# Moving softmax sums, Wo and VectorE's MLP work to other slots of an attention schedule written out by hand

## The chip, the core and the metric

The kernel runs on one core of a Trainium2 chip. The metric is the device time of one execution in microseconds (us); lower is better. The engines that matter are TensorE (PE in the profile; PEld is its weight load), VectorE (DVE), ScalarE (ACT), GpSimd (POOL) and SyncE (SP). SP and POOL issue most of the DMA transfers. Each engine works through its own instructions in order; they meet at semaphores only.

## What is computed

With x of 2048 tokens by 512, 32 heads of 128, 2048 cached keys and values per head, and an MLP of inner width 1792:

```python
xn = layernorm(x)
# A: attention over a cache
q = (xn @ wq) in heads
p = softmax(q @ k_cache^T * 128 ** -0.5)
s = concat(p @ v_cache) @ wo
# B: mixer MLP
h = gelu(layernorm(xn) @ w1)
hs = (h, its four quarters shifted by +1, -1, +2, -2 tokens) @ w2
x1 = xn + hs
b = x1 + gelu(layernorm(x1) @ w3) @ w4
out = x + s * silu(b)
```

Everything in HBM is bf16; sums in PSUM are fp32; gelu is the tanh form.

## The kernel before

Attention is cut into 128 **units** of one head by 512 queries: eight groups of four heads, in each four blocks of queries, in each the four heads (`units`). A unit has eight **slots** (`SPU`). The main loop counts slots (n = 8u + p) and writes into each slot, by hand, what every engine gets; `pin` keeps that order on the engine, so the order of the program is the order of the work.

In slot p of unit u:

- `s_slot`: two score matmuls (tile ps_s, two buffers) for 256 keys, then one exp on ScalarE (L168) into half of a tile pT.
- `pv_slot`: two matmuls of probabilities by values (ps_o), five slots behind the scores (`LAG`).
- slots 0 and 1, `q_mm`: four matmuls of the next unit's queries (ps_q); slot 2, `q_copy`: VectorE takes them to SBUF (L155).
- VectorE adds up the exp tiles for the softmax sums: `add_first` in slot 4 (L174), `add_next` in slot 6 (L179), `add_last` in slot 0 of the next unit (L179, L184, L185).
- slot 3 of the next unit, `sums`: four matmuls with a column of ones (ps_sum), reciprocal on VectorE (L204), and a store of 2 KB to DRAM on SP's queue (dr, L206). Slot 4, `bcast`: SP reads it back spread over all partitions (rb, L210). Slot 2 of the unit after, `norm`: VectorE multiplies ps_o by rb into oT (L218).
- slots 4 and 5, `wo_mm`: two halves of one output projection (ps_wo, four matmuls in all) for a block whose four heads are normalized; slot 6, `wo_post`: VectorE adds it to s_acc (L244, L246), in the last head group also the final product and the store (L250, L252, L253).
- slots 2, 3 and 6, 7: one **chunk** of the MLP, two matmuls or more in each of the two slots (ps_m, one buffer). There are 136 chunks for 236 such windows, so most units have one: m1 (w1, with GELU), m2 (w2), m3 (w3, with GELU), m4 (w4). The chunk's later steps are put on a list for coming slots with `at(n, step)`, where n is the slot of the chunk's second half, 3 or 7 within a unit. They come at the end of their slot.

ps_q, ps_sum and ps_wo share one PSUM buffer (pool `psX`, tag `xa`): each waits until VectorE has read the one before.

The steps of two GELU chunks (`gelu_pair`) are: square on ScalarE at n+1 (L286), poly on VectorE at n+3 (L290), tanh on ScalarE at n+5 (L295), last on VectorE at n+7 (L298). m2 has x1 on VectorE at n+1 (L357) and statistics at n+2 (L363, L364); m4 has x2 on VectorE at n+1 (L451), tanh on ScalarE at n+3 (L455) and silu on VectorE at n+5 (L458). The second layernorm (`ln2`) is applied at n+8, 10, 12, 14 on VectorE (L393), each with a DMA transpose on SP (L396).

SP's queue also carries the transposing loads of K (`load_k`, L128): in the last four units of each head group but the last, two pieces in slot 5 and two in slot 7, at the top of the slot, ahead of what the slot has of attention. V, the weights and the stores between stages go through POOL's queue.

Of the kernel before, what the change touches and what calls it, by code (L numbers as in the profile page):

```python
# [17 lines left out]
def kernel(  # L18
# [35 lines left out]
    SPU = KC // 2  # L54
# [50 lines left out]
    def mm(out, lhsT, rhs, start, stop):  # L105
        pin(nc.tensor.matmul(out=out, lhsT=lhsT, rhs=rhs, start=start, stop=stop))  # L106
# [7 lines left out]
    NU = len(units)  # L114
# [4 lines left out]
    def at(n, fn):  # L119
        todo[n].append(fn)  # L120


    def load_k(h, pieces):
        w = Sk // KSPLIT
# [98 lines left out]
    def wo_mm(g, t, hhs):  # L223
        if hhs[0] == 0:
            wo_box[0] = psX.tile([P, D], FP32, tag="xa", name="ps_wo")
        oT = oTs[(g, t // 4)]
        ts = t % 4
        for hh in hhs:
            mm(wo_box[0][:], oT[:, hh, ts * P:(ts + 1) * P], wos[g * HG + hh][:], hh == 0, hh == HG - 1)
# [51 lines left out]
    def gelu_pair(pre, dest, n):  # L281
        sq = gtp.tile([P, 2, 512], BF16, name="sq")
        f2 = "p a f -> p (a f)"

        def square():
            pin(nc.scalar.activation(  # L286
                out=sq[:], in_=pre[:], func=ACT.Square, scale=GELU_A ** 0.5))

        def poly():
            pin(nc.vector.scalar_tensor_tensor(  # L290
                out=sq[:].rearrange(f2), in0=sq[:].rearrange(f2), scalar=1.0,
                in1=pre[:].rearrange(f2), op0=ALU.add, op1=ALU.mult))

        def tanh():
            pin(nc.scalar.activation(out=sq[:], in_=sq[:], func=ACT.Tanh, scale=GELU_C))  # L295

        def last():
            pin(nc.vector.scalar_tensor_tensor(  # L298
                out=dest, in0=sq[:], scalar=1.0, in1=pre[:], op0=ALU.add, op1=ALU.mult))

        at(n + 1, square)
        at(n + 3, poly)
        at(n + 5, tanh)
        at(n + 7, last)

    def gelu_chunk(lhs, rhs, j, key, dest):
        def run(i, n):
# [36 lines left out]
    def m2_chunk(t):  # L344
        def run(i, n):
            if i == 0:
                mlp["ps"] = psX.tile([P, 512], FP32, tag="xm", name="ps_m")
                mlp["xr"] = tokp.tile([P, D], BF16, tag="tb", name="xr")
                nc.gpsimd.dma_start(out=mlp["xr"][:], in_=xn_d[t][:])
            for jc in (2 * i, 2 * i + 1):  # L350
                c0 = BASE_J[jc] + t * P - SHIFT[jc]
                mm(mlp["ps"][:], hT[:, jc, c0:c0 + P], w2_sb[:, jc, :], jc == 0, jc == DC - 1)
            if i == 1:
                ps, xr = mlp["ps"], mlp["xr"]

                def x1():
                    pin(nc.vector.scalar_tensor_tensor(  # L357
                        out=xr[:], in0=ps[:], scalar=0.5, in1=xr[:], op0=ALU.mult, op1=ALU.add))
                    nc.gpsimd.dma_start(out=x1_d[t][:], in_=xr[:])

                def stats():
                    bn = smp.tile([P, nc.vector.BN_STATS_DIM], FP32, name="bn")
                    pin(nc.vector.bn_stats(out=bn[:], in_=xr[:]))  # L363
                    pin(nc.vector.bn_aggr(out=mv2[:, t, :], in_=bn[:]))  # L364
                    rsqrt(rstd2[:, t:t + 1], mv2[:, t, 1:2])

                at(n + 1, x1)
                at(n + 2, stats)
        return run

    def ph2_open():
# [8 lines left out]
    def ln2(c, n):  # L380
        def start():
            mlp["xn2T"] = mp.tile([P, DC, 512], BF16, name="xn2T")
            xs = []
            for ts in range(4):
                xr = tokp.tile([P, D], BF16, tag="ta", name="x1r")
                nc.gpsimd.dma_start(out=xr[:], in_=x1_d[c * 4 + ts][:])
                xs.append(xr)
            mlp["xs"] = xs

        def apply(ts):  # L390
            t = c * 4 + ts
            xr = mlp["xs"][ts]
            pin(nc.vector.tensor_scalar(  # L393
                out=xr[:], in0=xr[:], scalar1=mv2[:, t, 0:1], scalar2=rstd2[:, t:t + 1],
                op0=ALU.subtract, op1=ALU.mult))
            pin(nc.sync.dma_start_transpose(  # L396
                out=mlp["xn2T"][:, :, ts * P:(ts + 1) * P], in_=xr[:]))

        at(n, start)
        for ts in range(4):  # L400
            at(n + 8 + 2 * ts, lambda ts=ts: apply(ts))

    def m3_chunk(c, fc):
        def dest():
# [28 lines left out]
    def m4_chunk(t, part):  # L433
        fcs = list(M4[part])
        ts = t % 4

        def run(i, n):
            if part == 0 and i == 0:
                mlp["ps"] = psX.tile([P, 512], FP32, tag="xm", name="ps_m")
                mlp["xr"] = tokp.tile([P, D], BF16, tag="tb", name="xr")  # L440
                nc.gpsimd.dma_start(out=mlp["xr"][:], in_=x1_d[t][:])
            h = (len(fcs) + 1) // 2
            for fc in (fcs[:h], fcs[h:])[i]:
                mm(mlp["ps"][:], mlp["h2"][fc // 2][:, fc % 2, ts * P:(ts + 1) * P],
                   mlp["w4"][fc][:], fc == 0, fc == FC - 1)
            if part == 2 and i == 1:
                ps, xr = mlp["ps"], mlp["xr"]
                th = tokp.tile([P, D], BF16, tag="th", bufs=1, name="th")

                def x2():  # L450
                    pin(nc.vector.scalar_tensor_tensor(  # L451
                        out=xr[:], in0=ps[:], scalar=0.5, in1=xr[:], op0=ALU.mult, op1=ALU.add))

                def tanh():
                    pin(nc.scalar.activation(out=th[:], in_=xr[:], func=ACT.Tanh, scale=0.5))  # L455

                def silu():
                    pin(nc.vector.scalar_tensor_tensor(  # L458
                        out=xr[:], in0=th[:], scalar=1.0, in1=xr[:], op0=ALU.add, op1=ALU.mult))
                    nc.gpsimd.dma_start(out=g_d[t][:], in_=xr[:])  # L460

                at(n + 1, x2)
                at(n + 3, tanh)
                at(n + 5, silu)
        return run

    chunks = deque()
# [47 lines left out]
    wo_todo = deque()  # L515
    for n in range(NS + 3 * SPU):
        u, p = divmod(n, SPU)
        if u < NU:
            g, qt, hh = units[u]
            if g + 1 < NG and qt == QT - 1:  # L520
                h = (g + 1) * HG + hh
                if p == 5:
                    load_k(h, (0, 1))
                elif p == 6:
                    load_v(h)
                    load_w(h)
                elif p == 7:
                    load_k(h, (2, 3))
                    load_wo(h)
            s_slot(u, p)  # L530
        m = n - LAG
        if 0 <= m < NS:
            pv_slot(*divmod(m, SPU))
        if p in (0, 1) and u + 1 < NU:
            q_mm(u + 1, (2 * p, 2 * p + 1))
        if p == 0 and 1 <= u <= NU:
            add_last(u - 1)
        if p == 2 and u + 1 < NU:
            q_copy(u + 1)
        if p == 2 and 2 <= u <= NU + 1:  # L540
            norm(u - 2)
            if units[u - 2][2] == HG - 1:
                gg, qq = units[u - 2][:2]
                wo_todo.extend((gg, 4 * qq + ts) for ts in range(4))
                if gg == NG - 1:
                    fin_load(4 * qq)
        if p == 3 and 1 <= u <= NU:
            sums(u - 1)
        if p == 4 and 1 <= u <= NU:
            bcast(u - 1)  # L550
        if p in (4, 5) and wo_todo:
            wo_mm(*wo_todo[0], (0, 1) if p == 4 else (2, 3))
        if p == 6 and wo_todo:
            gg, t = wo_todo.popleft()
            wo_post(gg, t)
            if gg == NG - 1 and t % 4 < 3:
                fin_load(t + 1)
        if p == 4 and u < NU:
            add_first(u)
        if p == 6 and u < NU:  # L560
            add_next(u, 2)
        if p in (2, 3, 6, 7):
            w = 2 * u + (p >= 4)
            i = p % 2
            if i == 0:
                want = -(-(w + 1 - W0) * NCH // (W1 - W0)) if w >= W0 else 0
                window.pop("run", None)
                if done < min(want, NCH):
                    if done in hooks:
                        hooks.pop(done)(n)  # L570
                    window["run"] = chunks.popleft()
                    done += 1
            if "run" in window:
                window["run"](i, n)
        for fn in todo.pop(n, ()):
            fn()
# [37 lines left out]
```

## Time and profile before

| | us |
|---|---|
| three timed runs | 1322.03, 1326.29, 1327.14 |
| their median | 1326.29 |
| the profiled execution | 1323.47 |
| its span, first to last instruction | 1321.7 |
| busy in it: PE, ACT, DVE | 1270.7, 1112.5, 1024.5 |
| mean granted TensorE clock | 0.991 |

The page counts an engine's busy time as a union of its instructions. Matmuls are pipelined: one of 128x512 shows some 380 ns, but the next starts 0.216 us after it. So a delay of TensorE is read from starts, not from gaps. In the list of waits a row says who waited, for whom, how long in all, how often and the longest.

### The profile page before, as it was taken

How to read it: one execution, taken by the hardware profiler on the slowest of the kernel's cores; microseconds unless marked ns; L12 is line 12 of the kernel's file. 1: busy time of each engine (PE TensorE's matmuls, PEld its weight loads, DVE VectorE, ACT ScalarE, POOL GpSimd, SP SyncE). 2: the span in 40 equal slices, each digit the busy share in tenths (PEclk: the TensorE clock that was granted, in tenths of full speed). 3: DMA queues.
4: the chain of work that ended last, by engine and by line, in shares of the span. 5: the costliest groups of instructions: out<-in, count | busy, mean ns of one | idle time of the engine just before them, and what ended most of it. 6: DMA issues, size and time to landing. Idle time of an engine off the chain costs nothing.

```text
span 1321.7 us, 17163 instructions
## 1 busy us (share of the span) xinstructions
PE 1270.7 (96%) x6208; PEld 575.4 (44%) x6208; DVE 1024.5 (78%) x1402; ACT 1112.5 (84%) x1185; POOL 220.2 (17%) x356
## 2 busy tenths in 40 slices
PE   3899999999999999999999999999999999999995
PEld 1344444444444444444444444444444444444442
DVE  1898788888787877788877777888777888777886
ACT  2799988778999988899988889998888999888882
POOL 6630122333211021100111011001010100000101
PEclk9899999999999999999999999999999999999997
DMA  9741373234823267222652127423292312712223
GB/s 217 189 102 27 53 140 84 72 85 112 151 57 70 55 116 124 61 41 44 127 114 60 48 49 121 96 56 65 62 146 57 64 33 48 132 29 52 81 67 88
DMA packets 144468, 112.29 MB, mean 85 GB/s; under 512 B 112320, under 2 KB 114880, under 8 KB 144384
## 3 DMA queue, kind: packets, MB, share of 16 engines
q1 hardware_dynamic: 126496, 57.19, 25.0%
q0 software_dynamic: 17600, 53.76, 15.8%
q8 instruction: 48, 0.79, 0.3%
q14 instruction: 36, 0.29, 0.1%
q10 hardware_dynamic: 288, 0.26, 0.1%
HBM read 81.53 MB, written 8.65 MB: 68 GB/s over the span
## 4 chain that ended last, share of the span: by engine, by line
PE 79%; DVE 9%; ACT 6%; DMA 3%; issue 2%; POOL 1%; DVEq 0%; POOLq 0%; SPq 0%
PE ps_s L106 29%; PE ps_o L106 27%; PE ps_m L106 8%; PE ps_wo L106 8%; PE ps_q L106 6%; ACT pT L168 4%; DVE acc L179 3%; PE ps_sum L106 1%; DVE acc L184 1%; DVE qT L155 1%; ACT sq L286 1%; DMA rb<-dr 1%; DMA xin<-in_A_x_dram 1%; ACT pre L316 1%; DVE gl L250 1%
## 5 line engine op out<-in xcount | busy, mean ns | idle before, releaser
L168 ACT ACTIVATE pT<-ps_s 128x1024 bf16<-128x1024 f32 x1024 | 1015.8, 1029 | 183.0 <-PE ps_s L106 179.0
L106 PE MATMUL ps_s<-qT,kT 128*128 128x512 bf16 x2048 | 611.2, 380 | 5.0 <-DVE qT L155 2.7
L106 PE MATMUL ps_o<-pT,vb 128*128 128x512 bf16 x2048 | 610.0, 380 | 0.0
L179 DVE TENSOR_TENSOR acc<-acc,pT 128x2048 bf16<-128x2048 bf16 x256 | 312.5, 1221 | 75.2 <-ACT pT L168 70.0
L106 PEld LDWEIGHTS <-vb 128*128 128x128 bf16 x2048 | 200.0, 98 | 243.0 <-issue 1.9
L106 PEld LDWEIGHTS <-kT 128*128 128x128 bf16 x2048 | 196.4, 98 | 244.2 <-issue 26.8
L174 DVE TENSOR_TENSOR acc<-pT 128x2048 bf16<-128x2048 bf16 x128 | 156.0, 1219 | 30.9 <-ACT pT L168 30.8
L106 PE MATMUL ps_q<-xnT,wq_h 128*128 128x512 bf16 x512 | 153.9, 383 | 20.7 <-DMA xnT<-xn 20.7
L106 PE MATMUL ps_wo<-wo_h,oT 128*128 128x512 bf16 x512 | 155.2, 387 | 7.4 <-DVE s_acc L246 3.1
L246 DVE TENSOR_TENSOR s_acc<-ps_wo,s_acc 128x512 f32<-128x512 f32 x112 | 77.3, 690 | 97.9 <-PE ps_wo L106 97.9
L155 DVE CAST qT<-ps_q 128x512 bf16<-128x512 f32 x128 | 87.3, 682 | 12.3 <-PE ps_q L106 12.3
L184 DVE TENSOR_TENSOR acc<-acc 128x1024 bf16<-128x1024 bf16 x128 | 88.6, 692 | 4.4
L218 DVE TENSOR_TENSOR oT<-ps_o,rb 128x512 bf16<-128x512 f32 x128 | 87.2, 681 | 4.6 <-DMA rb<-dr 4.5
L106 PEld LDWEIGHTS <-wq_h 128*128 128x128 bf16 x512 | 50.3, 98 | 81.9 <-DMA wq_h<-in_A_wq_dram 20.7
L106 PEld LDWEIGHTS <-oT 128*128 128x128 bf16 x512 | 50.6, 99 | 73.4 <-issue 14.5
L106 PE MATMUL ps_m<-xn2T,w_sb 128*128 128x512 bf16 x224 | 66.5, 378 | 0.0
L428 POOL DMA_DIRECT2D w_sb<-in_B_w_dram x28 | 21.2, 757 | 264.0 <-PE ps_m L106 235.1
L106 PE MATMUL ps_m<-w_sb,h2T 128*128 128x512 bf16 x224 | 63.9, 379 | 0.0
L139 POOL DMA_DIRECT2D wq_h<-in_A_wq_dram x32 | 24.5, 767 | 219.7 <-PE ps_q L106 217.1
L185 DVE TENSOR_TENSOR acc<-acc 128x512 bf16<-128x512 bf16 x128 | 54.4, 425 | 4.4
L106 PEld LDWEIGHTS <-acc 128*128 128x128 bf16 x512 | 37.2, 116 | 45.7 <-issue 14.7
L134 POOL DMA_DIRECT2D vb<-in_A_v_cache_dram x32 | 37.4, 1167 | 114.9 <-PE ps_o L106 104.6
(51 smaller groups left out, 607.1 us busy)
## 6 DMA issues: line engine op xcount, KB each, us to landing
rb<-dr SPq DMA_DIRECT2D x128, 256.0 KB, 4.1
vb<-in_A_v_cache_dram POOLq DMA_DIRECT2D x32, 512.0 KB, 7.1
w_sb<-in_B_w_dram POOLq DMA_DIRECT2D x28, 256.0 KB, 4.4
wq_h<-in_A_wq_dram POOLq DMA_DIRECT2D x32, 128.0 KB, 3.1
wo_h<-in_A_wo_dram POOLq DMA_DIRECT2D x32, 128.0 KB, 4.3
kT<-in_A_k_cache_dram SPq DMA_TRANSPOSE x128, 4.8
xn_d<-xn POOLq DMA_DIRECT2D x16, 128.0 KB, 3.9
dr<-rc SPq DMA_DIRECT2D x128, 2.0 KB, 1.5
```

What stands on the lines that cost most here:

```text
L106: pin(nc.tensor.matmul(out=out, lhsT=lhsT, rhs=rhs, start=start, stop=stop))
L134: nc.gpsimd.dma_start(out=vBs[h][:], in_=A_v_cache[0, h].rearrange("(kc p) d -> p kc d", p=P))
L139: nc.gpsimd.dma_start(out=wqs[h][:], in_=wq_v[:, :, h * Dh:(h + 1) * Dh])
L155: pin(nc.vector.tensor_copy(out=qT[:], in_=st[u].pop("psq")[:]))
L168: pin(nc.scalar.activation(out=s["pT"][-1][:, jj:jj + 2, :], in_=sps[:], func=ACT.Exp, scale=SCALE))
L174: pin(nc.vector.tensor_tensor(out=s["acc"][:], in0=s["pT"][0][:], in1=s["pT"][1][:], op=ALU.add))
L179: pin(nc.vector.tensor_tensor(out=a[:], in0=a[:], in1=st[u]["pT"][i][:], op=ALU.add))
L184: pin(nc.vector.tensor_tensor(out=a[:, 0:2, :], in0=a[:, 0:2, :], in1=a[:, 2:4, :], op=ALU.add))
L185: pin(nc.vector.tensor_tensor(out=a[:, 0, :], in0=a[:, 0, :], in1=a[:, 1, :], op=ALU.add))
L218: pin(nc.vector.tensor_tensor(out=oTs[(g, qt)][:, hh, :], in0=s["o"][:], in1=s["rb"][:], op=ALU.mult))
L246: pin(nc.vector.tensor_tensor(out=sa, in0=ps[:], in1=sa, op=ALU.add))
L428: nc.gpsimd.dma_start(out=w[:], in_=w3_v[:, :, fc * P:(fc + 2) * P])
```

## The change

The sums move from slot 3 to 4, their broadcast from slot 4 to 5, the two halves of Wo from slots 4 and 5 to 5 and 6; `wo_post` stays in slot 6, after the second half. VectorE's statistics, layernorm applies and silu are rounded up to the next slot 3, 5 or 7 (`soft`); x1 and x2 come in the chunk's own slot if that is slot 7, else one slot later as before (`evict`); GELU's poly, tanh and last come at n+4, n+6, n+8.

```diff
+    def soft(n):
+        while n % SPU not in (3, 5, 7):
+            n += 1
+        return n
+
+    def evict(n):
+        return n if n % SPU == SPU - 1 else n + 1
...
         at(n + 1, square)
-        at(n + 3, poly)
-        at(n + 5, tanh)
-        at(n + 7, last)
+        at(n + 4, poly)
+        at(n + 6, tanh)
+        at(n + 8, last)
...
-                at(n + 1, x1)
-                at(n + 2, stats)
+                at(evict(n), x1)
+                at(soft(n + 2), stats)
...
         for ts in range(4):
-            at(n + 8 + 2 * ts, lambda ts=ts: apply(ts))
+            at(soft(n + 8 + 2 * ts), lambda ts=ts: apply(ts))
...
-                at(n + 1, x2)
+                at(evict(n), x2)
                 at(n + 3, tanh)
-                at(n + 5, silu)
+                at(soft(n + 5), silu)
...
-        if p == 3 and 1 <= u <= NU:
+        if p == 4 and 1 <= u <= NU:
             sums(u - 1)
-        if p == 4 and 1 <= u <= NU:
+        if p == 5 and 1 <= u <= NU:
             bcast(u - 1)
-        if p in (4, 5) and wo_todo:
-            wo_mm(*wo_todo[0], (0, 1) if p == 4 else (2, 3))
+        if p in (5, 6) and wo_todo:
+            wo_mm(*wo_todo[0], (0, 1) if p == 5 else (2, 3))
         if p == 6 and wo_todo:
             gg, t = wo_todo.popleft()
             wo_post(gg, t)
```

## The prediction

> **What bounds the kernel.** I read the busy shares first, then PE's waits, then the timeline of single units. A unit (one head, 512 queries) has eight slots; numbers below are slot numbers, U is the start of a unit's first score matmul.
>
> The page's first part and clock row:
>
> ```profile
> PE 1270.7 (96%) x6208; PEld 575.4 (44%) x6208; DVE 1024.5 (78%) x1402; ACT 1112.5 (84%) x1185; POOL 220.2 (17%) x356
> ...
> PE   3899999999999999999999999999999999999995
> ...
> PEclk9899999999999999999999999999999999999997
> ```
>
> TensorE is the bound: 5696 matmuls of 128x512 that start 0.216 us apart when nothing holds them take 1230 us alone. So only PE's waits can be won, and only new ones lost. PE's waits over the whole span:
>
> ```profile
> PE ps_q L106 <- DMA xnT<-xn: 20.7, 1, 20.7
> PE ps_sum L106 <- DVE qT L155: 9.7, 15, 3.6
> PE ps_wo L106 <- DVE s_acc L246: 3.1, 4, 0.8
> PE ps_s L106 <- DVE qT L155: 2.7, 2, 1.9
> PE ps_wo L106 <- DVE oT L218: 2.5, 1, 2.5
> PE ps_sum L106 <- DVE acc L185: 2.5, 2, 2.2
> ```
>
> The first is the start. The second is what the change aims at: the sums in slot 3 need the one `xa` PSUM buffer, which q_copy frees in slot 2. A modelled matmul hides the first 0.16 us of a wait, so I counted delays from start to start in the timeline: up to the tail the sums lose 14.7 us (unit 1 alone 3.76), Wo in slot 4 3.4 us, and scores that wait for an exp some 11 us, mostly in pieces of 0.1 to 0.2. One such wait, DVE and PE at the end of slot 3 of unit 22:
>
> ```profile
> 251.32 0.68 DVE L357 SCALAR_TENSOR_TENSOR xr<-ps_m,xr 128x512 bf16<-128x512 f32 x1
> 252.04 0.69 DVE L363 BATCH_NORM_STATS2 bn<-xr 128x6 f32<-128x512 bf16 x1
> 252.77 0.18 DVE L364 BATCH_NORM_AGGREGATE mv<-bn 128x2 f32<-128x6 f32 x1
> 252.87 0.66 DVE L155 CAST qT<-ps_q 128x512 bf16<-128x512 f32 x1
> ```
>
> ```profile
> 252.49 0.59 PE L106 MATMUL ps_o<-pT,vb 128*128 128x512 bf16 x2
> 253.58 0.27 PE L106 MATMUL ps_sum<-ones_t,acc 128*128 128x1 bf16 x4 [0.50 <-DVE qT L155]
> ```
>
> The columns are start, duration, engine, line. After two ps_o the sums could start at 252.49 + 0.43 = 252.92; they start at 253.58, when the copy's 252.87 + 0.66 is over: 0.66 lost. x1 and the statistics (1.55 us by starts) stand ahead of the copy.
>
> **Part by part.** No arithmetic is added or removed; instructions move.
>
> *Slot lengths.* Scores and PV take 0.863 us, each pair of other matmuls 0.43, the sums 0.125. Before, slots 4 and 5 carry Wo; now 5 and 6. Wo's second half stands in slot 6 ahead of the MLP pair. So from the end of Wo to the next sums PE does the same work as before: six slots of scores and PV, two q pairs, the MLP pairs (old slots 6 to 3, new 6 to 4). **Where VectorE is gated by Wo's result (s_acc, L246), the shift alone wins nothing**: everything moves by one slot. It wins where VectorE is gated by an exp, or by what the second edit takes off the road.
>
> *MLP stage 2 (160 to 330 us).* Trace it through a unit with MLP in slots 6, 7 (unit 23). New Wo's second half starts at U+7.46; s_acc started 0.63 us after it before (255.87, 256.50), so U+8.09. By steps between starts: s_acc 0.61, add 1.14 gives x1 at 9.84; its matmul is out at 9.81, so the new wait in slot 7 is nothing. Queued behind x1 is the add of the last exp tile, ready at 10.03; it starts at 10.56. Then 1.26 + 0.72 + 0.34 gives q_copy at 12.88, done at 13.54. The sums come at U+9.62+5.18 = 14.80: 1.2 us to spare. Behind the copy come norm 0.60 and stats 0.82; the reciprocal could run at 14.87 and waits for the sums until 15.1; Wo starts at 15.79. The waits of units 17, 18, 22, 23, 24, 25, 29 go: 0.66+0.23+0.66+0.66+0.98+0.23+0.66 = **4.1 us**. Unit 16's (0.85 + 0.83) I keep: there the last GELU step and the statistics both stand before its reciprocal, so Wo waits. Wo of unit 30 (1.24, a late rb) I count at **0.9**; ends 0 and 1.24.
>
> *Six units (47, 52, 67, 72, 92, 112)* lose 0.20 at the sums (silu, 0.68, ahead of the copy) and 0.12 in slot 1 (tanh after short slots 6 and 7). Silu goes to slot 3 or 5, slot 6 gets longer: **1.9 us**.
>
> *Last units.* Unit 120's 0.83 falls to the 0.34 of its successors (silu again): **0.5**. The 0.34 of units 121 to 126 is the s_acc loop and stays.
>
> *Start.* Unit 1's sums wait 3.76 us because VectorE stands behind a load (DMA xin, 9.6 us). One slot later the wait is 2.9. After it PE runs at half speed (starts 0.427 apart) up to 48.2; the windows view gives a clock of 1.00 in 30 to 40 us and 0.66 in 40 to 50. A 2.0 us wait ending at 34.5 left full speed, the 3.76 us one did not; 2.9 lies midway. I take full speed, at little better than even odds. That is worth 2.7 to PE (13 matmuls, 0.21 late each), but only the 1.8 for which VectorE waited for the exp before 49.66. Units 2 and 4 lose 0.26 and 1.02; VectorE is nearly full there (9.9 of 10 us in 60 to 70), so 0.7 of it. Together **2.5**, ends 0.7 and 4. The 0.86 of lead is given back at the end, where s_acc of unit 127 comes 0.86 later and the last adds follow it.
>
> The Trainium skill, "TensorE: Matmul & The Clock Gate", The HAM clock gate, says that the clock halves after one idle window of about 3.4 us. The row with 3.76 us agrees, the tail's half speed after a 2.3 us wait does not; by the rule 2.9 us would keep the clock and the sum stays; by the tail's row the sum below is 1.8 less.
>
> *ScalarE.* A score matmul waits for the exp two slots back. From its start to the exp's end is 1.75 us by the rows (0.69 to the exp's start, 1.02, 0.04), exps follow each other at 0.905, a GELU tanh adds 0.95. Unit 9 shows the squeeze with the tanh in slot 0:
>
> ```profile
> 119.77 1.07 ACT L295 ACTIVATE sq<-sq 128x1024 bf16<-128x1024 bf16 x1
> ...
> 120.72 3.79 ACT L168 ACTIVATE pT<-ps_s 128x1024 bf16<-128x1024 f32 x4
> ...
> 121.80 0.59 PE L106 MATMUL ps_s<-qT,kT 128*128 128x512 bf16 x2
> 121.81 0.10 PEld L106 LDWEIGHTS <-kT 128*128 128x128 bf16 x1 [0.33 <-issue]
> ```
>
> Loss 0.22. With the tanh in slot 1 and slots 2, 3 bare (no sums in 3), the slack before slot 3 is 1.295+0.863-1.75 = 0.41, then 0.41+0.863-1.855 = -0.58. By the chunk schedule five pairs end in slot 3 with that pattern after them (units 8, 15, 34, 41, 100); unit 16 hides its own. They lost 0.1 to 0.2 before, so 0.38 more, four times: 1.5. Thirteen pairs that end in slot 7 with bare slots 2, 3 after them lose 0.05 each in slot 4 (0.905 against 0.863): 0.7. **Cost 2.2**, ends 0 and 4.
>
> *SyncE and DMA.* In the built program's order the broadcast rb passes behind two K transposes in 28 units (four per head group but the last), which it preceded before; the reciprocal's store dr stays ahead. Before:
>
> ```profile
> 173.37 0.32 SPq L206 DMA_DIRECT2D dr<-rc  x1
> 174.78 0.32 SPq L210 DMA_DIRECT2D rb<-dr  x1
> 175.15 6.12 SPq L128 DMA_TRANSPOSE kT<-in_A_k_cache_dram  x4
> ```
>
> Two transposes hold SP until dr+2.75 (1.1 and 1.3 us); rb went at dr+1.4 to 3.5 in these units before, so it is 0 to 1.3 us later, but with two transposes behind it in place of four. It took 3.9 to 7.7 there, mostly 5 to 6, and 4.1 in the median of all. So rb lands at dr+6.9 to 9.5, likely 7.3. Norm needs it at 13.45 against dr at 5.7, or 7.8 later, and 0.75 us more is covered, by VectorE's wait for the sums (15.1 - 14.87) and Wo's spare 0.5. Price nothing in most units; I take **0.7**, ends 0 and 27 (28 times 0.95). The V load from POOL's queue runs beside it as before.
>
> The Trainium skill speaks against this edit: "DMA: Bandwidth & Descriptors", Queues, rings and completion order, says a ring's descriptors are consumed in order, so rb could not overtake the transposes. Before, no rb stands behind a transpose issued just ahead of it, so the trace is silent. By the rule rb waits for the second transpose, issued at dr+1.5 and landed 4.8 later by the median, and the sum stays; with the slowest landing of these units (6.7) all 28 would be late and the sum about zero.
>
> *Sum*: 4.1+0.9+1.9+0.5+2.5 = 9.9 won, 2.2+0.7 lost: **7.0 us**. The profiled execution took 1323.47 (span 1321.7, 1.8 around it), so 1316.5 for its like; the median of the three runs shown, 1326.29, lies 2.8 higher, and from it 1319.3. That is the forecast.
>
> *At nothing*: GELU's poly, tanh and last step one slot later (the first reader of the result is at least one chunk, four slots, on; without it one slot, 1.3 us, per pair), and layernorm 2's applies with their four transposes on SP one to three slots later (eight stage-2 or twelve stage-4 chunks hide them; without these up to 3.9 us, four times). x1 and x2 in slot 7 free the MLP's PSUM buffer earlier, which no matmul waited for.
>
> **Rivals.**
> 1. *The wait only changes its name.* The closed loop through s_acc, reciprocal and Wo is the real limit, Wo waits where the sums did, and the start stays at half speed. For: VectorE waits 97.9 us for Wo before L246, and that loop is as long as before. Against: it waits 70.0 us for exps before L179, in stage 2 above all (0.96 ahead of the add at 259.28). Won 4.1/2 + 1.9 + 0.7 = 4.7, lost 2.2 + 0.7: gain 1.8, 1324.5.
> 2. *More is won.* Stage 2 in full (7.0 with units 16 and 30), start 4, rest 2.4, ScalarE free: gain 13, 1313.
> 3. *Slower: rb behind the transposes.* If it lands more than 8.55 us after dr, norm is late, the reciprocal behind it on VectorE too, and Wo waits. At the worst bound, dr+9.5, each of 28 units loses 0.95, 27 us; less the 7.7 won otherwise, 1345; with half the units, 1332. For: rb took up to 7.7 once and Wo then waited 1.24. Against: norm had over 1 us to spare in most units.
>
> **Numbers.** Forecast case (gain 4.5 to 10) 0.50; rival 1 0.28; rival 2 0.12; rival 3 0.10. The range 1311 to 1327 leaves out rival 3 and the rim of rival 2. A measurement tells 0.5%, 6.6 us: 1319.7. Of the forecast case 0.36 lies beyond it, with rival 2 faster 0.48; same 0.14+0.28 = 0.42; slower 0.10.
>
> **What will show it.** In the waits, ps_sum on qT falls from 9.7 to under 5 us, with none in stage 2; clock near 1.00 in 40 to 50 us; ps_s waits of some 0.5 us in slot 4 of units 9, 35, 42, 101; ps_sum waits of 0.34 (0.2 in the view) from unit 121 on. Wrong if ps_wo on rc or oT on rb grow to several us, or the sums' wait stays.

## The result and the profile after

The changed kernel takes **1330.48 us** (median of 7 runs, 1328.08 to 1333.55); the kernel before, beside it, 1322.03 (7 runs, 1321.20 to 1327.14). The ratio is 1.0055, 95% interval 1.0040 to 1.0069: slower by some 7 to 8 us, where 7.0 faster was forecast. The profiled execution took 1333.55 (span 1331.4), the longest of the seven.

The page's busy line and the two rows of slices, in the order shown of before:

```profile
PE 1265.0 (95%) x6085; PEld 576.1 (43%) x6208; DVE 1013.6 (76%) x1402; ACT 1108.3 (83%) x1185; POOL 223.8 (17%) x356
...
PE   3899999999999999999999999999999999999995
...
PEclk9999999999999999999999999999999999999996
```

TensorE is still the bound and its work is the same. (This trace lacks 123 of the 6208 matmul records; where one is missing, the next seems 0.216 us late, with nothing that released it.) VectorE is busy 76% instead of 78% of a longer span. The waits of PE over the whole span tell more:

```profile
PE ps_o L106 <- DVE oT L225: 7.8, 8, 1.8
PE ps_s L106 <- ACT pT L175: 5.1, 15, 0.7
PE ps_wo L106 <- DVE rc L211: 4.4, 9, 0.8
PE ps_sum L106 <- DVE qT L162: 3.6, 3, 2.7
```

Line numbers are seven higher than before. The sums' wait for the query copy fell from 9.7 us in 15 places to 3.6 in 3, all three in the first 80 us: from there on the wait that the change aims at is gone. In its place stands a row that the kernel before does not have, PV (ps_o) waiting for norm (oT) 7.8 us. Wo's wait for the reciprocal rose to 4.4 us; before, it was

```profile
PE ps_wo L106 <- DVE rc L204: 1.7, 2, 1.1
```

Both hang on VectorE, whose own waits say why:

```profile
DVE rc L211 <- PE ps_sum L106: 88.4, 82, 2.5
DVE oT L225 <- DMA rb<-dr: 36.7, 24, 2.7
```

Before, these two were

```profile
DVE rc L204 <- PE ps_sum L106: 30.7, 51, 1.2
DVE oT L218 <- DMA rb<-dr: 4.5, 3, 2.2
```

The first row says that VectorE now comes to the reciprocal before the sums are there. The second is the one that costs: norm waits for rb. The prediction had named this row as a sign that it is wrong.

**Unit 22**, whose 0.66 us the prediction showed, in the changed kernel: VectorE's copy and statistics, and PE's sums.

```profile
251.02 0.68 DVE L162 CAST qT<-ps_q 128x512 bf16<-128x512 f32 x1
...
252.22 0.68 DVE L370 BATCH_NORM_STATS2 bn<-xr 128x6 f32<-128x512 bf16 x1
```

```profile
253.00 0.26 PE L106 MATMUL ps_sum<-ones_t,acc 128*128 128x1 bf16 x4
```

The statistics now stand behind the copy, the copy ends at 251.70, and the sums start 1.3 us after it without a wait (1.2 was predicted for unit 23, where it is 1.4).

**Where the time comes from.** I laid the start of each unit's first exp beside that of before. By unit 28 the changed kernel is 3.2 us ahead. Then it falls back in steps: it is level at units 48 to 60, 3.7 behind at 80, 7.8 at 84, 8.4 at 96, and 8.8 at the end. Nearly every step lies where the next head group's K is loaded (units 28 to 31, 44 to 47, 60 to 63, 76 to 79, 92 to 95), or in the few units behind it, where the norms of these units stand. Such a place is unit 78, whose dr and rb go in unit 79 and whose norm stands in unit 80. First SP's queue, then VectorE, then PE, last the windows view (its column behind the engines is the granted clock):

```profile
827.46 0.32 SPq L213 DMA_DIRECT2D dr<-rc  x1
827.87 3.34 SPq L135 DMA_TRANSPOSE kT<-in_A_k_cache_dram  x2
833.15 0.32 SPq L217 DMA_DIRECT2D rb<-dr  x1
```

```profile
838.30 0.69 DVE L225 TENSOR_TENSOR oT<-ps_o,rb 128x512 bf16<-128x512 f32 x1 [2.56 <-DMA rb<-dr]
...
840.04 0.18 DVE L211 RECIPROCAL rc<-ps_sum 128x4 f32<-128x4 f32 x1
```

```profile
839.04 0.59 PE L106 MATMUL ps_o<-pT,vb 128*128 128x512 bf16 x2 [1.62 <-DVE oT L225]
840.27 1.01 PE L106 MATMUL ps_wo<-wo_h,oT 128*128 128x512 bf16 x2 [0.63 <-DVE rc L211]
```

```profile
841.00:844.00 3.00, 3.00 (x10) 1.15 (x9) 0.63 (x2) 1.02 (x1) 0.00 (x0) 0.61 0.23 44
```

Read downwards: dr is issued, two transposes at once behind it; SP is free of them at 831.2, but dr lands only at 833.13, 5.7 us after its issue, and rb, which reads what dr wrote, goes at 833.15 and lands at 838.27. Norm stood ready since 835.74. PV of unit 80 needs the PSUM buffer that norm reads, and waits; the reciprocal stands behind norm on VectorE, so Wo waits; and the clock is 0.61 in the mean of the 3 us behind these gaps: the trace's clock record has half speed from 839.93, within the second gap, to 843.34. In the changed kernel rb lands 10.8 us after dr's issue. In the kernel before it landed 7.4 us after it, with dr down in 1.6:

```profile
822.73 0.52 SPq L206 DMA_DIRECT2D dr<-rc  x1
824.34 0.32 SPq L210 DMA_DIRECT2D rb<-dr  x1
```

### The profile page after: what moved, and what is told of

It is laid out like the page before. It is cut to its first block, busy times and chain, and to the rows that moved or that the text cites. A ratio compares the mean times of both kernels' runs of the same rounds, so it can differ in the third digit from the quotient of the medians.

```text
span 1331.4 us, 17063 instructions
## 1 busy us (share of the span) xinstructions
PE 1265.0 (95%) x6085; PEld 576.1 (43%) x6208; DVE 1013.6 (76%) x1402; ACT 1108.3 (83%) x1185; POOL 223.8 (17%) x356
## 4 chain that ended last, share of the span: by engine, by line
PE 73%; DMA 9%; DVE 8%; ACT 7%; issue 2%; SPq 1%; POOL 1%; DVEq 0%; ACTq 0%; POOLq 0%
PE ps_s L106 26%; PE ps_o L106 25%; PE ps_m L106 8%; PE ps_wo L106 8%; PE ps_q L106 6%; ACT pT L175 5%; DMA rb<-dr 4%; DMA dr<-rc 3%; DVE acc L186 2%; PE ps_sum L106 1%; ACT sq L293 1%; SPq L135 1%; DMA xin<-in_A_x_dram 1%; DVE acc L191 1%; ACT pre L323 1%
## 5 line engine op out<-in xcount | busy, mean ns | idle before, releaser
L106 PE MATMUL ps_s<-qT,kT 128*128 128x512 bf16 x2002 | 600.9, 380 | 10.1 <-ACT pT L175 5.1
L106 PE MATMUL ps_o<-pT,vb 128*128 128x512 bf16 x1999 | 598.4, 379 | 10.8 <-DVE oT L225 7.8
L106 PEld LDWEIGHTS <-kT 128*128 128x128 bf16 x2048 | 192.4, 98 | 231.2 <-issue 33.9
L181 DVE TENSOR_TENSOR acc<-pT 128x2048 bf16<-128x2048 bf16 x128 | 153.0, 1195 | 0.3
L211 DVE RECIPROCAL rc<-ps_sum 128x4 f32<-128x4 f32 x128 | 22.9, 179 | 88.5 <-PE ps_sum L106 88.4
L192 DVE TENSOR_TENSOR acc<-acc 128x512 bf16<-128x512 bf16 x128 | 54.4, 425 | 4.4
```

The source lines that it names most:

```text
L181: pin(nc.vector.tensor_tensor(out=s["acc"][:], in0=s["pT"][0][:], in1=s["pT"][1][:], op=ALU.add))
L192: pin(nc.vector.tensor_tensor(out=a[:, 0, :], in0=a[:, 0, :], in1=a[:, 1, :], op=ALU.add))
L211: pin(nc.vector.reciprocal(out=rc[:], in_=ps[:]))
```

## The experiments

The theory after this reading: **the two K transposes between dr and rb in 28 units cost what was lost and more; the rest of the change is a gain.** Rivals: the slots of the sums and Wo cost by themselves, or ScalarE's later tanh does. Each kernel was timed beside the kernel before in five rounds; ratios are to that, with 95% intervals.

### rb ahead of the transposes (e1)

```diff
-                if p == 5:
-                    load_k(h, (0, 1))
...
         if p == 5 and 1 <= u <= NU:
             bcast(u - 1)
+        if p == 5 and u < NU and g + 1 < NG and qt == QT - 1:
+            load_k((g + 1) * HG + hh, (0, 1))
```

> The changed kernel with one thing undone: in slot 5 the two K transposes are issued behind the broadcast rb, so that SP's order is dr, rb, four transposes as before the change. Theory (rb late behind the transposes): the waits of norm on rb fall from 36.7 us in 24 places to under 8 us, the waits of ps_o on norm go except at the start, and the time falls from 1330 by 10 to 15 us, to 2 to 8 us below the kernel before. Rival (the moved sums and Wo, or the shorter slots 3 and 4, cost the time by themselves): it stays within 3 us of the changed kernel, 5 to 9 us above the kernel before.

Measured: 1321.94 us (1319.33 to 1324.54, 12 runs), ratio 0.9986 [0.9973, 0.9998]. That is 8.5 us less than the changed kernel's median, or 0.69% by the two ratios, 9.1 us, where I expected 10 to 15. Norm still waits 14.6 us for rb, in 17 places; I expected under 8. SP in the same unit:

```profile
818.43 0.52 SPq L213 DMA_DIRECT2D dr<-rc  x1
821.75 0.32 SPq L217 DMA_DIRECT2D rb<-dr  x1
822.12 5.03 SPq L135 DMA_TRANSPOSE kT<-in_A_k_cache_dram  x4
```

PE's waits from 60 to 1230 us, past the start and ahead of the tail, for e1:

```profile
PE ps_s L106 <- ACT pT L175: 3.7, 11, 0.4
PE ps_wo L106 <- DVE rc L211: 1.2, 2, 0.8
PE ps_sum L106 <- DVE qT L162: 0.5, 1, 0.5
```

In that view the changed kernel has

```profile
PE ps_o L106 <- DVE oT L225: 6.0, 7, 1.6
PE ps_wo L106 <- DVE rc L211: 4.0, 8, 0.8
```

with ps_s at 4.1 and ps_sum at 0.4. PV's wait is gone, Wo's mostly. So this order is the cause of the loss. But the kernel is only 1.8 us faster than before, at the low end of the 2 to 8 that I expected.

### Each part alone (e2, e3, e4)

e2 is the kernel before with the broadcast alone in slot 5, behind the transposes; e3 has the first edit alone, e4 the second alone (`soft`, `evict`, GELU one slot later).

```diff
-        if p == 4 and 1 <= u <= NU:
+        if p == 5 and 1 <= u <= NU:
             bcast(u - 1)
```

> The kernel before with one thing changed: the broadcast rb is issued in slot 5, behind the two K transposes, and sums and Wo stay in slots 3 to 5. Theory: rb lands 1 to 3 us later in 28 units; norm has 0 to 2 us more room than in the changed kernel, so the price is smaller than there but clear: 4 to 12 us above the kernel before. Rival: the place of rb in SP's queue is hidden, within 2 us of the kernel before.

Measured: 1329.11 us, ratio 1.0043 [1.0028, 1.0058]. Norm waits 20.0 us for rb (before 4.5), Wo 5.4 for the reciprocal (1.7). The order in SP's queue alone costs 5.4 us, with the sums still in slot 3.

> The first edit alone: sums, broadcast and Wo one slot later, VectorE's MLP work as before. Theory: the price of rb is in it, the win in MLP stage 2 mostly is not: as slow as the changed kernel or up to 5 us slower, 7 to 14 us above the kernel before. Rival (the second edit is what costs): within 3 us of the kernel before.

Measured: 1331.65 us, ratio 1.0069 [1.0049, 1.0089]; norm waits 33.6 us for rb. By unit 28 its profiled run is 5.7 us ahead, and it loses 11.6 from there to the end. So the win in stage 2, which I had expected to be missing here, is in it.

> The second edit alone: statistics, layernorm, silu and the GELU steps in slots 3, 5 and 7, x1 and x2 in slot 4 or 7, sums, broadcast and Wo as before. Theory: no K transpose passes rb, the waits of the sums in stage 2 shrink, 1 to 5 us below the kernel before. Rival (the later tanh and the new wait of x1 in slot 7 cost): 2 to 6 us above it.

Measured: **1317.37 us**, ratio 0.9956 [0.9939, 0.9973]. The second edit alone is 6.4 us faster than before, more than the 1 to 5 that I expected. Its waits of PE from 60 to 1230 us begin

```profile
PE ps_s L106 <- ACT pT L175: 3.0, 9, 0.4
PE ps_sum L106 <- DVE qT L162: 1.3, 1, 1.3
```

where the kernel before has

```profile
PE ps_sum L106 <- DVE qT L155: 5.0, 8, 0.9
```

The gains of the two edits don't add up: each by itself takes most of the sums' wait in stage 2 away.

### How many transposes, and where (e6, e8)

e6 is the changed kernel with one of the two pieces behind rb; e8 has both in slot 3, ahead of the sums, so that none lies between dr and rb.

```diff
-                if p == 5:
+                if p == 3:
                     load_k(h, (0, 1))
```

> The changed kernel with one of the two K pieces of slot 5 behind the broadcast instead of ahead of it: one transpose between dr and rb in 28 units. Theory (each transpose ahead of rb makes it later by its issue of 1.1 to 1.3 us and part of its landing; norm has some 1 us to spare): a little of the 8.5 us between two pieces and none stays, 1323 to 1326. Rival A (linear, half per piece): 1326.2. Rival B (any transpose issued right behind dr holds up dr itself, one is as bad as two): 1328 to 1331.

> The changed kernel with the two K pieces issued at the top of slot 3 instead of slot 5, so that both stand ahead of dr and none between dr and rb. Theory A (what counts is that nothing is issued between dr and rb, SP's own time): dr goes when the reciprocal is done, some 2 us after the second transpose was issued, rb 1.4 to 3 us later: 1321 to 1324 like the kernel with rb first. Rival B (transposes that are still landing, 4 to 7 us, hold up whatever store or load follows them): dr lands 3 to 5 us after its issue, rb follows late, 1327 to 1332.

Measured: e6 1325.96 us (1320.46 to 1332.63, 12 runs), ratio 1.0017 [1.0000, 1.0034]; e8 1321.03, ratio 0.9987 [0.9975, 1.0000]. One piece costs about half of two, which is rival A's 1326.2 to 0.2 us and lies just inside my 1323 to 1326; the spread of the runs does not part these. Transposes issued two slots ahead of dr cost no more than those behind rb (e8 and e1 have the same ratio); those issued between dr and rb do.

The traces show how. Of the 28 units with K loads, medians in us from dr's issue; "due" is when VectorE comes to norm and would start it if rb were there, "over" the sum of what rb lands later than due:

| kernel | transposes between | sums in slot | dr landed | rb issued | rb landed | norm due | late | over |
|---|---|---|---|---|---|---|---|---|
| before | 0 | 3 | 2.3 | 2.3 | 7.1 | 8.2 | 3 | 3.1 |
| e4 | 0 | 3 | 2.5 | 2.5 | 7.5 | 8.3 | 3 | 1.8 |
| e2 | 2 | 3 | 1.5 | 3.3 | 8.6 | 8.2 | 17 | 16.6 |
| e1 | 0 | 4 | 2.7 | 2.7 | 7.6 | 7.7 | 14 | 7.9 |
| e8 | 0 | 4 | 2.3 | 2.3 | 7.4 | 7.6 | 13 | 15.5 |
| e6 | 1 | 4 | 3.1 | 3.1 | 8.1 | 7.7 | 18 | 22.8 |
| e3 | 2 | 4 | 2.6 | 3.9 | 8.7 | 7.8 | 22 | 29.3 |
| after | 2 | 4 | 3.7 | 4.0 | 8.6 | 7.5 | 22 | 31.6 |

Each row is from one profiled run; that of e6, 1332.63, was the longest of its twelve. Two things meet. Transposes between dr and rb move rb's landing from 7.1 to 8.6: SP is held by them (e2, where rb goes some 1.8 us after dr is down), or dr itself comes down late (after, 3.7 against 2.3). And moving sums and dr by a slot while norm stays in slot 2 moves the due time from 8.2 to 7.5 or 7.7. Either alone makes some units late; both make 22 of 28 late.

Whether the two transposes right behind dr are what brings it down late is not shown. In the first of the four units with K loads in each head group, where no transpose is in flight from before, dr lands after 2.5 us (before) and 2.7 (e1) in the median with none behind it, and after 3.9 in the changed kernel, in e2 and in e3 with two. But e2 has the same order in all 28 units and 1.5 in their median, and e3 has 2.6.

PE has some slack of its own behind norm: from e1 to the changed kernel 23.7 us more of lateness became 8.5 of time, from before to e2 13.5 became 5.4.

### rb on another queue (e7)

```diff
-        pin(nc.sync.dma_start(
+        pin(nc.gpsimd.dma_start(
             out=st[u]["rb"][:], ...
```

> The changed kernel with the broadcast rb issued on POOL's queue in place of SP's; dr and the K transposes stay on SP in their order. Theory A (order in SP's queue is what makes rb late: the issue behind two transposes): rb goes as soon as dr has landed, waits of ps_o for norm go, 1322 to 1325, unless a V load (512 KB) that stands ahead of it in POOL's order takes its place as the obstacle. Rival B (dr itself lands late with transposes right behind it, and rb shares the DMA engines with them whatever queue it is on): rb still lands 10 us and more after dr's issue in the 28 units, time 1328 to 1332. POOL's statistics steps queue behind rb; that could cost up to 2 us more in stage 2.

Measured: 1398.29 us, ratio 1.0562 [1.0543, 1.0581], outside every expectation. On POOL's queue rb stands behind loads of V and weights that wait for their buffers: in units without K loads too it went up to 9.1 us after dr had landed, and PV waited 49.1 us for norm. It does not tell whether dr's late landing comes from SP's ring or from shared DMA engines; that stays open.

What the traces do tell is the order of landing. In the 14 traces 6080 pairs of SP's transfers are in flight together and end on different semaphores, so that each end is recorded by itself; in none does the later one land first. In the changed kernel rb lands at least 0.5 us behind the second transpose in all 28 units, and within 0.8 us of it in 11 (in unit 78 the transpose lands at 837.72, rb at 838.27); in e2 it is within 0.8 in 17. Between queues the order does not hold: in e7, with rb on POOL's queue, rb lands ahead of the second transpose in 9 of the 28. So on SP's queue a slow transpose ahead of rb sets the earliest time at which rb lands, beside SP's time for issuing it.

### Room for norm (e9)

e9 is the changed kernel with `norm` called in slot 3 instead of 2.

> The changed kernel with norm in slot 3 instead of slot 2; the K transposes stay between dr and rb. Theory (the first edit moved dr and rb one slot later but left norm in slot 2, so that the time from dr to norm shrank by about a slot, and a late rb then holds VectorE with the next sums' reciprocal behind it): some 0.7 us more room, the waits of norm for rb fall from 36.7 us to under 20, the time from 1330.5 to 1324 to 1327. Rival (PE waits for the normalized values themselves, for psO in slot 5 and for Wo, wherever norm stands in VectorE's order): 1329 to 1332.

Measured: 1329.66 us, ratio 1.0042 [1.0028, 1.0057], and norm waits 38.8 us for rb. The rival was right. In all 28 units VectorE has nothing else between the copy and norm, so norm comes at nearly the same time (due at 7.6, against 7.5 in the changed kernel) whether the program writes it in slot 2 or 3. A slot is a place in an order, not a time.

### The second edit taken apart (e5, e11), and the first relieved (e10, e12)

e5 is e4 with GELU's three steps back at n+3, n+5, n+7; e11 is the kernel before with m2's statistics alone moved, from slot 1 to 3.

```diff
-                at(n + 2, stats)
+                at(soft(n + 2), stats)
```

> The second edit alone, but with GELU's poly, tanh and last step back at n+3, n+5, n+7: only x1, x2, statistics, layernorm applies and silu move. Theory (ScalarE's squeeze from the later tanh is the loss inside the second edit): the stalls of 0.54 us in five units and of 0.39 after the sums in four fall to the 0.1 to 0.2 of the kernel before, so about 2.3 us less than the 1317.4 measured for the second edit alone: 1315, range 1313 to 1317, and no return of sums waits in units 17 to 29. Rival (the later GELU steps are part of the win, because poly and last stood ahead of the copies on VectorE): the sums' waits come back in part and the time is 1319 to 1321.

> The kernel before with one thing moved: the statistics of m2 chunks that end in slot 7 go from slot 1 to slot 3, behind the copy of the next queries. Theory (the 0.82 us of statistics ahead of the copy are what the sums waited for in stage 2): the sums' waits of units 17 to 29 go and some 4.5 to 5.5 us are won by unit 32, nothing after: 1318 to 1320. Rival (x1 in slot 0, which stays, or the loop through s_acc holds the sums anyway): 1321 to 1324.

Measured: e5 **1315.74 us** (1315.21 to 1318.11), ratio 0.9944 [0.9929, 0.9960], the fastest kernel here, 8.0 us under the kernel before. Its waits of PE from 60 to 1230 us are

```profile
PE ps_wo L106 <- DVE rc L211: 1.1, 2, 0.6
PE ps_sum L106 <- DVE qT L162: 1.0, 2, 0.9
PE ps_s L106 <- ACT pT L175: 0.6, 2, 0.4
```

so ScalarE's 3.0 of e4 are gone to 0.6, as expected; the time fell by 1.6 where I expected 2.3, and the intervals of e4 and e5 overlap. e11: 1320.49, ratio 0.9980 [0.9967, 0.9992], 2.6 faster than before. In its trace 4.3 us are won from unit 16 to 28 and 0.8 given back by unit 32 to an rb that was late once. One line carries most of stage 2, a little less than expected.

e12 is e8 with GELU back at the old slots; e10 has norm in slot 3 as well.

> The kernel with the second edit and GELU back (1315.7 measured) plus the first edit freed of its obstacles: the two K pieces in slot 3, norm in slot 3. Theory (the later sums win nothing once statistics and silu are out of the copy's way, and give 0.9 to 1.0 back at the end): 1316 to 1319. Rival A (the later sums do win at the start and at the end of stage 2 once rb is in time): 1311 to 1315. Rival B (the shorter time from dr to norm costs in all units, transposes or not): 1319 to 1322.

> The changed kernel with the two K pieces in slot 3 (1321.0 measured) and GELU back at n+3, n+5, n+7; norm stays in slot 2. It parts the 6.6 us by which the kernel with norm in slot 3 as well was slower. Theory (with the sums in slot 4 the old tanh, in slot 4 for pairs that end in slot 7, meets the shortest place of ScalarE's slack; in the trace of that kernel scores lost 3.6 us more to exps): 1323.5 to 1325.5. Rival A (norm in slot 3 is the loss): 1320 to 1322. Rival B (both GELU and norm are nothing by themselves, the difference was the chip or the start): 1320 to 1322 with no more waits of scores for exps than 13.1 us.

Measured: e10 1327.68 us, ratio 1.0039 [1.0023, 1.0056]; e12 1327.72, ratio 1.0033 [1.0020, 1.0046]. Both miss their expectations upwards. Norm in slot 3 is worth nothing that the ratios show, and with the sums in slot 4 the old GELU slots, which win 1.6 us in e5, cost 6.7 (e12 against e8; 6.1 by the ratios). Scores wait longer for exps in e12:

```profile
PE ps_s L106 <- ACT pT L175: 6.3, 22, 0.6
```

against 4.6 us in 15 places in e8. By starts, without the places where a record is missing, these delays grew from 11.1 to 13.5 us from unit 2 on, and from unit 12 to unit 127 the profiled run of e12 falls 2.5 us behind that of e8. So the later GELU belongs to the first edit: with sums in slot 4 the old tanh slots hold up scores in more places. The other 3.6 to 4.2 us I can't place: the profiled runs differ most at the start, up to 6 us from the first loads, and I have no way to part that from GELU.

## Why the prediction was wrong

*The step that failed* is the one on SyncE and DMA: "So rb lands at dr+6.9 to 9.5, likely 7.3 ... Price nothing in most units; I take **0.7**". The mechanism was named, as rival 3, with the point from which it decides; its size was wrong. The term measured 8.5 (after against e1), and that leaves out what the 14 norms still late in e1 cost. Three things in it:

- rb's issue. I took dr+2.75, the time of two transposes, and treated dr, which "stays ahead", as unmoved. Measured: dr lands at 3.7 in the median and up to 5.7 (2.3 before), rb goes at 4.0. I had priced only SP's time, and not that dr could come down later than before.
- rb's flight with fewer transposes behind it was foreseen: 4.4 us against 5.2 before. But the second transpose came down at 7.3 in the median and up to 10.3, and rb never ahead of it: rb landed at 8.6 in the median, up to 10.8.
- The room. From unit 23 I took 7.8 and added 0.75 of slack. Over the 28 units it was 7.5, and 8.2 before: I read one unit, in a stage where VectorE is late, for all.

And the price per late unit: I named Wo's wait. PV's wait for the PSUM buffer that norm reads (6.0 us from 60 us on) was not in the text at all, nor was the half clock after it.

The Trainium skill's rule that I weighed there, "DMA: Bandwidth & Descriptors", Queues, rings and completion order, that a ring's descriptors are consumed in order, spoke against the edit, and its worse reading ("all 28 would be late and the sum about zero") was nearer than mine: 22 were late. The traces agree with it on SP's queue, where no transfer landed ahead of one issued before it. The trace of the kernel before was not silent on this: in 52 pairs dr was issued while a transpose ahead of it was in flight, and it never landed first.

*What held.* Stage 2 and unit 30's Wo: 4.1 + 0.9 predicted, 5.3 measured in e1 from unit 16 to unit 31, with no wait of the sums left; unit 16's Wo wait stayed (0.93), as said. The five pairs of units 9, 16, 35, 42 and 101 lose what the sum says, 0.544 us each against 0.58; I had counted four of them, without unit 16. Unit 9 again:

```profile
122.18 0.59 PE L106 MATMUL ps_s<-qT,kT 128*128 128x512 bf16 x2 [0.38 <-ACT pT L175]
```

The sums of units 121 on kept 0.30 (0.34 predicted). The lead given back at the end is 1.0 (0.86).

*What came otherwise* (read in e1). The six units won their 1.9, since silu is out of the way. But in six others (44, 49, 69, 89, 94, 114) a score behind the sums now waits 0.44 us for an exp, 2.7 lost that the sum does not have. Against that the 0.166 us waits of the 13 pairs that end in slot 7 vanished, 2.2 us that the sum does not have either; the waits in slot 4 that I put at 0.05 each are 0.09, 1.2 in all. The start (2.5 predicted) is 0.4 at unit 12 of the changed kernel's profiled run, but 2.1 in e8's, whose first twelve units are the same program: it varies from run to run. The clock in 40 to 50 us did come out at 1.00 instead of 0.66, on which that term rested, but this was luck. e9 has the same program up to there and the same wait, and runs at half speed behind it; first the changed kernel, then e9:

```profile
42.62 0.26 PE L106 MATMUL ps_sum<-ones_t,acc 128*128 128x1 bf16 x4 [2.70 <-DVE qT L162]
42.75 0.59 PE L106 MATMUL ps_s<-qT,kT 128*128 128x512 bf16 x2
```

```profile
42.69 0.27 PE L106 MATMUL ps_sum<-ones_t,acc 128*128 128x1 bf16 x4 [2.70 <-DVE qT L162]
42.82 1.01 PE L106 MATMUL ps_s<-qT,kT 128*128 128x512 bf16 x2
```

In the changed kernel's profiled run the wait moved on: norm of unit 0 comes at 53.70, as before, because its rb lands then; PE gets there sooner and waits, and the half clock follows:

```profile
54.44 0.63 PE L106 MATMUL ps_o<-pT,vb 128*128 128x512 bf16 x2 [1.80 <-DVE oT L225]
54.87 1.05 PE L106 MATMUL ps_s<-qT,kT 128*128 128x512 bf16 x2
...
58.28 0.60 PE L106 MATMUL ps_o<-pT,vb 128*128 128x512 bf16 x2
```

Matmuls run some 0.427 apart from 54.9 to 58.3, as they did from 43 to 48.2 before. I had not asked what PV waits for next.

With rb first (e1) the forecast, without its rb term, was 7.7; the medians show 1.8. That is rival 1's number but not its mechanism: Wo's wait for the reciprocal is 1.2 us in e1 and 1.7 before. In e1's profiled run 5.9 are won from unit 1 to unit 127, where half of the 28 norms are still late, and 1.0 is given back at the end; that run's first loads put unit 1 2.1 us late, and such starts differ between runs of one kernel. The difference between 7.7 and 1.8 I could not place in full. Moving the sums is not what wins: the second edit without it wins 6.4, and 8.0 with its GELU part left out. With rb first, the first edit on top of the second still costs 4.0 us by the ratios (e1 against e4), so the rival that its slots cost by themselves was right in part.

## What to carry to other kernels

When a store and the load that reads it back are moved in a queue, take their whole round trip against its due time in every unit of the kind that gets something new between them, not in one, expect the load to land behind whatever the queue carries ahead of it, and measure the store's own landing with its new neighbours. When a producer moves a slot later and its consumer stays, the room shrinks by that slot: both must be counted. And when several waits go with one edit, try its parts alone: here one line (the statistics behind the copy) won 2.6 us by itself, the second edit 6.4, and the first, alone, cost 7.9.

## What the runs showed of the hardware

- A 2 KB store landed in 1.5 us in the median of the changed kernel's 100 units without K loads, and in 3.7, up to 5.7, where two DMA transposes were issued right behind it. That these are the reason is not shown (e2: the same order, 1.5 in the median). Transposes issued some two slots ahead of it left it at 2.3 in the median, up to 5.5 (e8).
- Transfers of SP's queue landed in the order of issue in all 6080 pairs in flight together in the 14 traces. Transfers of different queues did not: rb on POOL's queue landed ahead of SP's second transpose in 9 of 28 units (e7).
- The issue of one transposing load held SP for 1.1 to 1.3 us in most cases, now and then for 1.4 to 3.7 (after).
- PE's clock halved around gaps of 1.80 us (54.4) and of 1.62 and 0.63 (839 to 840), while a wait of 2.70 us for the sums of unit 1 left it at full speed in the changed kernel and halved it in e9. The Trainium skill, "TensorE: Matmul & The Clock Gate", The HAM clock gate, gives one idle window of about 3.4 us, free-running; in these runs the length of a single gap does not decide it. The clock records do show a fixed grid: in each of the 14 traces any two changes of the clock lie a whole multiple of 3.41 us apart. By my estimate from the matmuls' starts (0.216 us each) the clock halved, between 30 and 1296 us, behind every such stretch in which PE was busy for 0.36 of the time or less, and behind none with more than 0.39 (28 halvings, some 5100 others). The 2.70 us wait left the two stretches that it spanned in the changed kernel busy for 0.50 and 0.58; in e9 it fell into one, busy for 0.25.
